# Attention and token mixer on one core: the two o visits of a straddling stretch, and the bank that the second one opens

## The chip, the core and the metric

The kernel runs on one core of a Trainium2 chip. The core has five engines with a queue each: TensorE (PE, matmuls; its weight loads are shown apart as PEld), VectorE (DVE), ScalarE (ACT), GpSimd (POOL) and SyncE (SP, which issues the DMAs). Matmuls write PSUM, which has eight banks of 128 x 512 fp32 values; only DVE and ACT read it here. The metric is the device time of one execution in microseconds, the median of three runs.

## The reference

Two branches over the same x (2048 x 640), mixed by a gate for each row. Cut to what matters:

```python
# A: 32 heads of 20, one shared k and v
q = (x @ wq).reshape(B, S, H, Dh).transpose(0, 2, 1, 3); k = x @ wk; v = x @ wv
p = softmax(einsum("bhqd,bkd->bhqk", q, k) * Dh ** -0.5)
a = einsum("bhqk,bkd->bhqd", p, v).transpose(0, 2, 1, 3).reshape(B, S, H * Dh) @ wo
# B: token mixer
u = gelu(einsum("bsd,sf->bdf", layernorm(x), w1) + b1)
b = (einsum("bdf,fs->bds", u, w2) + b2).transpose(0, 2, 1)
g = sigmoid((x * gate_w).sum(-1, keepdims=True))
out = g * a + (1 - g) * b          # S = 2048, D = 640, F = 1728
```

## The kernel before

After a prologue (layer norm, projections, the first B columns) one long loop does the rest. Attention is cut into 32 **query groups** n (four heads by 512 queries) and 16 key blocks kb of 128 keys; a **unit** in the code's list `units` is one pair (n, kb), 512 in all. For each unit there are four score matmuls (`qk`, line 668), each of which fills one PSUM bank; ACT reads the bank and writes the exponentials into an SBUF tile `p` (line 674). A **visit** (`pv_mm`, line 701) then multiplies the four p tiles of a unit by v and adds the products into the four 32-partition quarters of one bank, the o bank. The profile counts eight matmul records for a visit. Visits of kb 0 to 15 add into the same bank; the visit with kb = 0 starts it afresh, and after kb = 15 ACT copies it to SBUF (line 714, `on<-o`). The rest of that evacuation (transposes, division, a split in two, DMAs) is put off in the list `later` and handed out by `settle`, a piece at a time. When the text below says that a visit "opens the next group", it means a visit with kb = 0; the change's title calls the group of sixteen visits a unit.

The row maxima of a later group are computed ahead with the same kind of matmul (`ms_next`, line 479), each into one bank that DVE reduces (line 482).

**Banks.** Score and row maximum matmuls take banks in turn from `next_bank`: three of the pool `ps_m` (name `ms`) and three of `ps_s` (name `s`), alternately, so each bank comes round after six matmuls. `ring[0]` is the bit that alternates. A call makes a new tile in a pool's oldest slot, and its first writer waits until the old tile's reader is done. The seventh bank is `ps_g` for the matmuls of branch B and of the output projection (`g`), the eighth is `ps_o` for o.

**Order.** The program order is written out by hand. The loop runs over 326 **stretches** (`ph`, function `main`). Even and odd stretches use opposite halves of the PE rows: scores and maxima of half b are interleaved with some 15 to 17 `g` matmuls of the other half, so that two row halves work at once. A visit uses all 128 rows and four groups of 32 columns instead. An even stretch ends with one visit, an odd one with two back to back: three visits in two stretches (below: a **pair** of stretches). So `vs` holds one or two units, and `wide` says that it holds two. Since 16 is no multiple of 3, the two visits of an odd stretch are kb = 15 of one group and kb = 0 of the next every 48 units: units 15 and 16, 63 and 64, and so on to 447 and 448, ten times. There `parted` is true, and the first visit is moved to the middle of the stretch (line 1066), so that ACT can copy the o bank while the second half of the stretch runs and the second visit can open the same bank at its end.

The last 24 visits come after the loop in blocks of two, with four banks for scores (`s_banks`) and three for the projection's last jobs (`a_free`).

Of the kernel before, what the change touches and what calls it, by code (L numbers as in the profile page):

```python
# [9 lines left out]
F32 = mybir.dt.float32  # L10
# [7 lines left out]
P = 128  # L18
S, D, H, DH, F = 2048, 640, 32, 20, 1728
NS = S // P  # L20
# [4 lines left out]
NB = 512  # L25
# [14 lines left out]
def mix_kernel(ctx: ExitStack, tc: tile.TileContext, A_x, A_wq, A_wk, A_wv, A_wo,  # L40
# [5 lines left out]
    def f32(ap):  # L46
        return ap.bitcast(F32)
# [402 lines left out]
    ps_m = ctx.enter_context(tc.tile_pool(name="ps_m", bufs=3, space=PSUM))  # L450
# [6 lines left out]
    ring = []  # L457

    def next_bank():
        if not ring:  # L460
            return ps_m.tile([P, NB], F32, name="ms")
        ring[0] ^= 1
        return ps_m.tile([P, NB], F32, name="ms") if ring[0] else ps_s.tile([P, NB], F32, name="s")
    given = [0, 0]
    issued = [0, 0]

    def ms_next(b):
        k = given[b]
        if k >= 32 * NU:
            return None  # L470
        given[b] += 1
        n, r = divmod(k, 32)
        (kq, pr), qt = divmod(r // 4, 2), r % 4

        def step():
            if n not in mtiles:
                mtiles[n] = mpool.tile([P, 16, 4], F32, name="mp")
            ms = next_bank()
            nc.tensor.matmul(ms, qmax[n][64 * b:64 * b + 60, pr, qt * P:(qt + 1) * P],  # L479
                             kst[64 * b:64 * b + 60, kq * NB:(kq + 1) * NB], start=True, stop=True)  # L480
            c = (2 * b + pr) * 4 + qt
            nc.vector.tensor_reduce(mtiles[n][:, c, kq:kq + 1], ms, axis=AX.X, op=ALU.max)  # L482
            issued[b] += 1
            if min(issued) == 32 * n + 1:
                new_qmax(n + 1)

        return step
# [18 lines left out]
    def fetch_max(n):  # L506
        src = m_scr[n].rearrange("(i j b r) e -> j b r i e", j=2, b=2, r=8)
        for b in range(2):
            for j in range(2):
                rows = f32(qtiles[n][64 * b + 60 + j:64 * b + 61 + j])  # L510
                nc.sync.dma_start(out=rows.rearrange("o p (t i e) -> o (p t) i e", i=4, e=32), in_=src[j, b][None])
# [48 lines left out]
    def pop_chain():  # L560
        f = chain.pop(0) if chain else None
        if f:
            f()
# [39 lines left out]
    ps_s = ctx.enter_context(tc.tile_pool(name="ps_s", bufs=3, space=PSUM))  # L603
    ps_o = ctx.enter_context(tc.tile_pool(name="ps_o", bufs=1, space=PSUM))
# [24 lines left out]
    units = [(n, kb) for n in range(NU) for kb in range(NS)]  # L629
# [8 lines left out]
    s_banks, s_turn, a_free = [], [0], []  # L638
# [6 lines left out]
    def s_next(b):  # L645
        j = sc[b]
        if j >= 2 * len(units):
            return None
        sc[b] += 1

        def step():
            qk(j // 2, j % 2, b)

        step.score = True
        return step
# [36 lines left out]
    otile = {}  # L692
    later = []

    def pv_mm(u):
        n, kb = units[u]
        if kb == 0:
            otile[0] = ps_o.tile([P, NB], F32, name="o")
        o = otile[0]
        for hh in range(4):  # L700
            nc.tensor.matmul(o[32 * hh:32 * hh + 32, :], v_sb[:, kb, :], ptiles.pop((u, hh)),  # L701
                             start=(kb == 0), stop=(kb == NS - 1), skip_group_check=True)
        if kb == NS - 1 and n < NU - 1:
            qb, g = divmod(n, NQ)
            ot = ev.tile([P, NB // 32, 32], F32, name="ot")
            rl = ev.tile([P, NB // 32], F32, name="rl")
            on = ev.tile([P, NB], F32, name="on")
            oh = ev.tile([P, NB], F32R, name="oh")
            ol = ev.tile([P, NB], F32R, name="ol")
            direct = spare[0]  # L710
            src = o
            if not direct:
                src = on
                nc.scalar.activation(src, o, AF.Copy)

            def turn():
                nc.vector.transpose(ot.rearrange("p c e -> p (c e)"), src)

            def scale():
                if not direct:  # L720
                    turn()
                nc.vector.reciprocal(rl, ot[:, :, DH])  # L722
                (nc.vector if spare[0] else nc.gpsimd).tensor_mul(ot, ot, rl[:, :, None].to_broadcast([P, NB // 32, 32]))  # L723

            if direct:
                turn()

            def back():
                nc.vector.transpose(on, ot.rearrange("p c e -> p (c e)"))

            def high():
                nc.gpsimd.tensor_copy(oh, on)

            def low():
                nc.gpsimd.tensor_sub(ol, on, f32(oh))
                for j, t in enumerate((oh, ol)):
                    for hh in range(4):
                        r = (4 * g + hh) * DH
                        nc.sync.dma_start(out=o_scr[j, r:r + DH, qb * NB:(qb + 1) * NB],
                                          in_=f32(t[32 * hh:32 * hh + DH, :]))  # L740

            if direct:
                later.append((False, None))
            later.extend(((True, scale), (True, back), (False, high), (False, low)))
# [268 lines left out]
    def merged(lx, lf):  # L1013
        lanes, at, out = (list(lx), list(lf)), [0.0, 0.0], []
        while lanes[0] or lanes[1]:
            k = 0 if lanes[0] and (not lanes[1] or at[0] <= at[1]) else 1
            us, f = lanes[k].pop(0)
            if f:
                out.append(f)
            at[k] += us  # L1020
        return out
# [5 lines left out]
    def settle(wide=False):  # L1027
        for _ in range(2 if spare[0] else 1):
            if later and (wide or spare[0] or not later[0][0]):
                f = later.pop(0)[1]  # L1030
                if f:
                    f()
        pop_chain()
# [6 lines left out]
    def main(k, vs):  # L1040
        b = k % 2
        fs, rest, done = ph[k]
        fill = [(F_US, f) for f in fs] + [(0.0, f) for f in [signal] + done]
        if not vs:
            lx = [(3 * X_US, ms_next(b)), (3 * X_US, ms_next(b)), (X_US, s_next(b)), (X_US, ms_next(b))]
            lx += [(X_US, s_next(b)) for _ in range(3)]
            lf = fill + [(X_US, s_next(1 - b))]
        else:
            sx, sf = (MANY if len(fs) > 15 else FEW)[len(vs) == 1]
            lx = [(X_US, (s_next if c == "s" else ms_next)(b)) for c in sx]  # L1050
            lf = []
            for c in sf:
                lf += fill if c == "F" else [(X_US, (s_next if c == "s" else ms_next)(1 - b))]
        order = merged(lx, lf)
        scores = [f for f in order if getattr(f, "score", False)]
        known, kept = set(row_max), set(sent)
        wide = len(vs) == 2
        parted = wide and units[vs[0]][1] == NS - 1
        hold = None
        if done and vs and not k + 1 >= len(ph) and k % 2 == 0 and len(fs) > 15:  # L1060
            hold = [i for i, f in enumerate(order[:order.index(done[0])]) if f in scores][-1]
        for i, f in enumerate(order):
            if wide and i == (len(order) + 1) // 2:
                settle()
                if parted:
                    pv_mm(vs[0])
            if i == hold:
                delayed.append(None)
            f()
            if hold is not None and f is done[0]:  # L1070
                delayed.pop(1)()
                delayed.clear()
        ms_done()
        spare[0] = len(row_max) == NU
        settle(wide and not parted)
        if vs:
            n, kb = units[vs[0]][0] + 1, units[vs[0]][1]
            if n in kept and n not in back_in:
                fetch_max(n)
                back_in.add(n)  # L1080
        for f in rest:
            f()
        if vs and kb > 4 and n in known and n not in sent and n < NU:
            store_max(n)
            sent.add(n)
        for v in vs[parted:]:
            pv_mm(v)

    ring.append(0)
    v = 0  # L1090
    for k in range(len(ph)):
        n = 0 if k == 0 else 1 + k % 2
# [8 lines left out]
    if NU - 1 not in sent:  # L1101
        store_max(NU - 1)

    s_banks.extend(ps_s.tile([P, NB], F32, name="s") for _ in range(3))
    s_banks.append(ps_m.tile([P, NB], F32, name="ms"))
    a_free.append(ps_g.tile([P, NB], F32, name="g"))
    a_free.extend(ps_m.tile([P, NB], F32, name="ms") for _ in range(2))
    assert not later
    for i in range(4):
        tail_load(NS - 4 - NA + i, late=True)  # L1110
# [1 line left out]
    for n in BLOCKS:  # L1112
# [3 lines left out]
        i = 0  # L1116
# [31 lines left out]
    o = otile[0]  # L1148
# [78 lines left out]
```

## Time and profile before

| | |
|---|---|
| median of three runs | 1662.53 us (1661.41 to 1663.34) |
| profiled execution | 1662.79 us, of which 1661.0 us are the span from the first to the last instruction |
| DVE busy | 1431.1 us, 86% of the span |
| ACT busy | 1188.1 us, 72% |
| POOL busy | 608.1 us, 37% |

The profile is that of one execution. An engine's busy time is the union of its instructions; a chain of waits follows the last instruction back through whatever released it. A timeline row gives the start, the length, the engine, the line, the tiles (written<-read), the shapes, the count, and in brackets the idle time of that engine ahead of it with what ended it. A row of a window table gives the bounds, the length, the busy time (and number of records) of the engines, the granted clock, the DMA share and GB/s.

### The profile page before, as it was taken

The numbers are of one execution on the slowest core, as the hardware profiler recorded it, in microseconds if no ns is written. First come the engines' busy times: TensorE is split into PE (matmuls) and PEld (weight loads), VectorE is DVE, ScalarE is ACT, GpSimd is POOL, SyncE is SP. The second block draws the span as 40 slices with busy tenths as digits, with TensorE's granted clock in tenths as the row PEclk, the third lists the DMA queues.
The fourth block names the chain that finished last, engine by engine and source line by source line (L and its number), as shares of the span: only waits on it lengthen the run. The fifth ranks groups of instructions, "written<-read, shape, count | busy, mean of one in ns | idle before, by whom it ended". The sixth has DMA issues, their size and how long they took to land.

```text
span 1661.0 us, 38834 instructions
## 1 busy us (share of the span) xinstructions
PE 1651.6 (99%) x14877; PEld 1104.0 (66%) x14877; DVE 1431.1 (86%) x2725; ACT 1188.1 (72%) x2349; POOL 608.1 (37%) x765
## 2 busy tenths in 40 slices
PE   9999999999999999999999999999999999999998
PEld 7889666666666666666666666666666666666655
DVE  6689889989989999998999899899899989988943
ACT  4444777777777777777777777777777777777775
POOL 6568545544464554522232322122222221111220
PEclk9999999999999999999999999999999999999999
DMA  7655222222233222222222222122221222333521
GB/s 210 206 168 144 75 70 68 78 64 78 60 78 78 71 74 68 58 72 67 67 75 61 58 65 67 56 66 67 67 61 55 67 66 64 99 107 97 165 82 38
DMA packets 178527, 138.60 MB, mean 83 GB/s; under 512 B 33369, under 2 KB 144118, under 8 KB 178342
## 3 DMA queue, kind: packets, MB, share of 16 engines
q1 hardware_dynamic: 178054, 135.80, 29.3%
q8 instruction: 117, 1.92, 0.5%
q14 instruction: 68, 0.56, 0.1%
q10 hardware_dynamic: 288, 0.33, 0.1%
HBM read 102.36 MB, written 31.65 MB: 81 GB/s over the span
## 4 chain that ended last, share of the span: by engine, by line
PE 97%; DVE 2%; ACT 1%; issue 0%; DVEq 0%; ACTq 0%
PE o L701 29%; PE ms L479 19%; PE s L668 14%; PE g L763 10%; PE g L952 7%; PE ms L668 4%; PE pp L298 4%; PE g L898 3%; PE pu L586 2%; PE s L479 2%; DVE mp L482 1%; ACT p L674 1%; PE pp L362 0%; PE pt L290 0%; PE ms L853 0%; DVE yo L529 0%
## 5 line engine op out<-in xcount | busy, mean ns | idle before, releaser
L482 DVE TENSOR_REDUCE mp<-ms 128x1 f32<-128x512 f32 x1576 | 1003.2, 685 | 129.9 <-PE ms L479 105.0
L674 ACT ACTIVATE p<-s 128x512 f32<-128x512 f32 x1551 | 845.6, 606 | 307.2 <-PE s L668 292.4
L479 PE MATMUL ms<-kst,qmx 60*128 60x512 f32 x1576 | 673.7, 433 | 2.6 <-DVE mp L482 2.6
L668 PE MATMUL s<-qst,kst 62*128 62x512 f32 x1551 | 612.3, 400 | 0.0
L701 PE MATMUL o<-p,v_sb 128*32 128x512 f32 x4096 | 511.4, 601 | 0.0
L479 PEld LDWEIGHTS ms<-kst,qmx 60*128 60x128 f32 x1576 | 290.6, 185 | 264.1 <-ACT p L674 109.4
L482 DVE TENSOR_REDUCE mp<-s 128x1 f32<-128x512 f32 x472 | 315.9, 684 | 8.5 <-PE s L479 8.3
L668 PEld LDWEIGHTS s<-qst,kst 62*128 62x128 f32 x1551 | 286.2, 186 | 43.7 <-DVE flag L688 23.5
L674 ACT ACTIVATE p<-ms 128x512 f32<-128x512 f32 x497 | 286.4, 600 | 39.2 <-PE ms L668 36.7
L952 PE MATMUL g<-slot,wh 64*128 64x320 f32 x1280 | 297.6, 312 | 0.0
L129 POOL TENSOR_TENSOR wl<-wr,wh 128x512 fp32r<-128x512 f32 x176 | 228.0, 1297 | 47.8 <-PE g L763 21.1
L701 PEld LDWEIGHTS o<-p,v_sb 128*32 128x32 f32 x4096 | 97.6, 108 | 184.6 <-issue 176.7
L952 PEld LDWEIGHTS g<-slot,wh 64*128 64x128 f32 x1280 | 211.6, 184 | 2.0 <-issue 1.7
L479 PE MATMUL s<-kst,qmx 60*128 60x512 f32 x472 | 208.2, 448 | 0.4 <-DVE yo L525 0.4
L763 PE MATMUL g<-slot,wh 64*128 64x320 f32 x864 | 201.5, 313 | 0.0
L763 PE MATMUL g<-u,wh 64*128 64x320 f32 x864 | 201.0, 313 | 0.0
L668 PE MATMUL ms<-qst,kst 62*128 62x512 f32 x497 | 199.9, 402 | 0.0
L952 PE MATMUL g<-slot,wl 64*128 64x320 f32 x640 | 199.6, 312 | 0.0
L128 POOL CAST wh<-wr 128x512 fp32r<-128x512 f32 x144 | 88.0, 611 | 222.5 <-PE g L763 114.5
L763 PEld LDWEIGHTS g<-slot,wh 64*128 64x128 f32 x864 | 143.3, 184 | 1.7 <-issue 1.7
L723 POOL TENSOR_TENSOR ot<-ot,rl 128x512 f32<-128x512 f32 x30 | 31.5, 1050 | 307.3 <-DVE rl L722 307.3
L763 PEld LDWEIGHTS g<-u,wh 64*128 64x128 f32 x864 | 143.1, 184 | 1.1 <-issue 1.1
(221 smaller groups left out, 2086.2 us busy)
## 6 DMA issues: line engine op xcount, KB each, us to landing
wr<-in_B_w_dram SPq DMA_DIRECT2D x152, 256.0 KB
qmx<-q_scr SPq DMA_DIRECT2D x192, 80.0 KB
qst<-q_scr SPq DMA_DIRECT2D x192, 80.0 KB
slot<-o_scr SPq DMA_DIRECT2D x22, 320.0 KB
y_scr<-yo SPq DMA_DIRECT2D x16, 320.0 KB
o_scr<-oh SPq DMA_DIRECT2D x124, 40.0 KB
o_scr<-ol SPq DMA_DIRECT2D x124, 40.0 KB
q_scr<-qh SPq DMA_DIRECT2D x19, 256.0 KB
```

Source lines behind the costliest of these rows:

```text
L128: nc.gpsimd.tensor_copy(wh, wr)
L129: nc.gpsimd.tensor_sub(wl, wr, f32(wh))
L298: nc.tensor.matmul(pp, w, t, start=first and n == 0, stop=not more and n == len(steps) - 1)
L479: nc.tensor.matmul(ms, qmax[n][64 * b:64 * b + 60, pr, qt * P:(qt + 1) * P], kst[64 * b:64 * b + 60, kq * NB:(kq + 1) * NB], start=True, s ...
L482: nc.vector.tensor_reduce(mtiles[n][:, c, kq:kq + 1], ms, axis=AX.X, op=ALU.max)
L586: nc.tensor.matmul(pu[r][:, :HD2], w[rows, c, :], h[rows, st, :], start=(st == 0 and k == 0), stop=(st == NS - 1 and k == 2))
L668: nc.tensor.matmul(s, kst[64 * b:64 * b + 62, kb * P:(kb + 1) * P], q[64 * b:64 * b + 62, pr, :], start=True, stop=True)
L674: nc.scalar.activation(p, s, AF.Exp, scale=SCALE)
L701: nc.tensor.matmul(o[32 * hh:32 * hh + 32, :], v_sb[:, kb, :], ptiles.pop((u, hh)), start=(kb == 0), stop=(kb == NS - 1), skip_group_check ...
L763: other_tile(half, nc.tensor.matmul(hold["p"][:, :HD2], w[r, fc % HS, :], u[d][r, fc, :], start=(hold["n"] == 1), stop=(hold["n"] == 6 * F ...
L898: other_tile(half, nc.tensor.matmul(hold["p"][:, :HD2], o[r, c, :], w[r, c, d * HD2:(d + 1) * HD2], start=(hold["n"] == 1), stop=(hold["n" ...
L952: other_tile(half, nc.tensor.matmul(hold["p"][:, :HD2], w[r, st % HS, :], h[d][r, st, :], start=(hold["n"] == 1), stop=(hold["n"] == 6 * NS)))
```

## The change

The ring becomes a list of six lasting tiles that are rotated, in place of new tiles from two pools. `otile[0]` is one tile as well, allocated once. In a wide stretch whose second visit has kb = 0, that visit calls `pv_mm` with `swap`: the present o bank goes to the young end of the ring, the oldest bank of the ring becomes the o bank. The parted form, with its visit in the middle of a stretch, is gone, and both visits stand at the end as in every other wide stretch. After the loop the six banks of the ring are handed to `s_banks` and `a_free` in the order of their age.

```diff
     def next_bank():
         if not ring:
             return ps_m.tile([P, NB], F32, name="ms")
-        ring[0] ^= 1
-        return ps_m.tile([P, NB], F32, name="ms") if ring[0] else ps_s.tile([P, NB], F32, name="s")
+        ring.append(ring.pop(0))
+        return ring[-1]
...
-    def pv_mm(u):
+    def pv_mm(u, swap=False):
         n, kb = units[u]
-        if kb == 0:
-            otile[0] = ps_o.tile([P, NB], F32, name="o")
+        if swap:
+            ring.append(otile[0])
+            otile[0] = ring.pop(0)
         o = otile[0]
...
         wide = len(vs) == 2
-        parted = wide and units[vs[0]][1] == NS - 1
...
             if wide and i == (len(order) + 1) // 2:
                 settle()
-                if parted:
-                    pv_mm(vs[0])
...
-        settle(wide and not parted)
+        settle(wide)
...
-        for v in vs[parted:]:
-            pv_mm(v)
-
-    ring.append(0)
+        for v in vs:
+            pv_mm(v, wide and v == vs[1] and units[v][1] == 0)
+
+    ring.extend((ps_s if i % 2 else ps_m).tile([P, NB], F32, name="s" if i % 2 else "ms") for i in range(6))
+    otile[0] = ps_o.tile([P, NB], F32, name="o")
...
-    s_banks.extend(ps_s.tile([P, NB], F32, name="s") for _ in range(3))
-    s_banks.append(ps_m.tile([P, NB], F32, name="ms"))
+    s_banks.extend(ring[:4])
     a_free.append(ps_g.tile([P, NB], F32, name="g"))
-    a_free.extend(ps_m.tile([P, NB], F32, name="ms") for _ in range(2))
+    a_free.extend(ring[4:])
```

## The prediction

> **What bounds the kernel now.** I read the engines' busy times first, then the chain of waits, then the timeline around single visits, and windows cut at visits.
>
> ```profile
> PE 1651.6 (99%) x14877; PEld 1104.0 (66%) x14877; DVE 1431.1 (86%) x2725; ACT 1188.1 (72%) x2349; POOL 608.1 (37%) x765
> ...
> PE 97%; DVE 2%; ACT 1%; issue 0%; DVEq 0%; ACTq 0%
> ```
>
> PE is busy for 99% of the span and carries 97% of the chain that ended last. A busy PE need not be a well used one: one row half can stand still while the other works, and the record shows no idle time. So PE's time has to be read as a pace, from one visit to the next. The timeline of PE shows a normal wide stretch (16 records of o in a row) and one of the ten straddling ones:
>
> ```profile
> 211.07 1.92 PE L701 MATMUL o<-p,v_sb 128*32 128x512 f32 x16
> ...
> 218.41 1.07 PE L701 MATMUL o<-p,v_sb 128*32 128x512 f32 x8
> ...
> 220.85 1.07 PE L701 MATMUL o<-p,v_sb 128*32 128x512 f32 x8
> ```
>
> Two visits back to back take 1.92 us, two apart 2 x 1.07 = 2.14. To see the whole price I cut windows from the start of an even stretch's visit to the start of the next even stretch's: a pair of stretches with three visits (24 records). The view is that of windows for line 701 alone; the length of a window is the pace. The ten straddling pairs:
>
> ```profile
> 215.82:224.89 9.07, 3.20 (x24) 0.47 (x24) 1.00 0.23 65
> 354.84:363.78 8.94, 3.20 (x24) 0.47 (x24) 1.00 0.16 47
> 493.73:502.67 8.94, 3.20 (x24) 0.47 (x24) 1.00 0.11 29
> 632.60:641.66 9.07, 3.20 (x24) 0.47 (x24) 1.00 0.25 56
> 772.21:781.41 9.21, 3.20 (x24) 0.47 (x24) 1.00 0.22 66
> 912.27:921.35 9.08, 3.19 (x24) 0.47 (x24) 1.00 0.46 133
> 1052.14:1061.08 8.94, 3.20 (x24) 0.47 (x24) 1.00 0.30 84
> 1191.92:1200.99 9.08, 3.20 (x24) 0.47 (x24) 1.00 0.24 56
> 1331.88:1340.81 8.94, 3.20 (x24) 0.47 (x24) 1.00 0.01 2
> 1470.05:1479.30 9.24, 3.20 (x24) 0.47 (x24) 1.00 0.34 97
> ```
>
> And pairs that do not straddle: first 15 of them in one window (360 records), then five single ones, then two of the last stage (the output projection):
>
> ```profile
> 224.89:354.84 129.95, 44.84 (x360) 8.63 (x360) 1.00 0.28 73
> 816.39:825.05 8.66, 2.99 (x24) 0.57 (x24) 1.00 0.29 85
> 868.65:877.46 8.81, 2.99 (x24) 0.57 (x24) 1.00 0.26 72
> 1096.06:1104.72 8.65, 2.99 (x24) 0.57 (x24) 1.00 0.31 84
> 1148.32:1157.13 8.81, 2.99 (x24) 0.58 (x24) 1.00 0.24 70
> 1288.27:1296.93 8.66, 2.99 (x24) 0.57 (x24) 1.00 0.29 68
> 1505.18:1513.77 8.59, 2.99 (x24) 0.57 (x24) 1.00 0.39 116
> 1513.77:1522.46 8.69, 2.99 (x24) 0.58 (x24) 1.00 0.20 56
> ```
>
> The granted clock is 1.00 in all of them, so the difference is not the clock. The kernel keeps a beat that the straddling pairs break. The five single windows lie at the same place of their five-pair job in the second B stage as the straddling pairs at 772, 912, 1052, 1192 and 1332, in this order; the place decides whether the beat there is 8.66 or 8.81. All five hold one of the other two kinds of group end (kb = 15 as the single visit, or as the second of a wide stretch), so an o copy as such does not break the beat in that stage.
>
> **The change, part by part.** *The visit in the middle goes.* A straddling pair should take the length of a pair without it. The first four go against 129.95 / 15 = 8.663: 9.07 + 8.94 + 8.94 + 9.07 - 4 x 8.663 = 1.37. The next five, each against its own place: 0.55, 0.27, 0.29, 0.27 and 0.28, together 1.66. The last against 8.59: 0.65, or 0.55 if a group's end costs its 0.10 there as in the window at 1513.77. Sum 1.37 + 1.66 + 0.65 = **3.68 us**, at least 3.58.
>
> The plain price is some 0.28 us: 0.22 for the parted visits, and the rest, as I take it, because one row half runs out before the other at one more place. The Trainium skill, TensorEngine Tiling (Array Packing), Key Properties, says that a change of tiling mode drains TensorE; its TensorE: Matmul & The Clock Gate, Single matmul latency, puts a drain at about 175 ns. My estimate from that page is 2 x 0.175 = 0.35 us for each additional excursion and 3.5 us for ten; the rows have 0.28 at the plain sites, below it, and more at others, and the measurement decides.
>
> At four sites more is lost. At the first, the timeline of ACT and the rows of line 952 around it say why:
>
> ```profile
> 219.57 0.60 ACT L714 ACTIVATE on<-o 128x512 f32<-128x512 f32 x1 [0.40 <-PE o L701]
> ...
> 221.49 0.55 ACT L519 ACTIVATE yo<-g,bias 128x320 f32<-128x320 f32 x1
> ```
>
> ```profile
> L952 PEldq EVENT_SEMAPHORE  x1: 321/321/321, 221.8 to 221.8; - x1
> ```
>
> The o copy in the middle of the stretch pushes ACT back by 0.6 us and its wait; then ACT empties the g bank only until 222.04, and the next job's first g matmul holds PE's queue for 0.32 us. With the copy behind the visits, the g bank is emptied ahead of it, so this goes too; it is already in the sum.
>
> *The o copy moves* behind the first visit. Above, ACT starts it 219.57 - 218.41 = 1.16 us after the visit's start. It would run from 1.16 to 1.76 us after the start of two joined visits. That time has to be free on ACT; where the last stage is busiest, ACT, DVE and PE show:
>
> ```profile
> 1386.96 1.10 ACT L674 ACTIVATE p<-ms 128x512 f32<-128x512 f32 x2
> 1387.91 0.63 ACT L674 ACTIVATE p<-s 128x512 f32<-128x512 f32 x1
> 1390.43 2.09 ACT L674 ACTIVATE p<-ms 128x512 f32<-128x512 f32 x4 [1.89 <-PE ms L668]
> ```
>
> ```profile
> 1389.42 0.68 DVE L482 TENSOR_REDUCE mp<-s 128x1 f32<-128x512 f32 x1
> ```
>
> ```profile
> 1388.04 1.92 PE L701 MATMUL o<-p,v_sb 128*32 128x512 f32 x16
> ...
> 1390.95 0.40 PE L668 MATMUL ms<-qst,kst 62*128 62x512 f32 x1
> ```
>
> ACT idles 1.89 us, from 0.50 to 2.39 after the visits' start at 1388.04. The copy fits there with 0.63 to spare, so I cost it at nothing; without the cover it would hold the next exponentials back by up to 0.60. Nothing of `later` moves: in a stretch that straddles the list is empty, and its first piece is taken at the end of the next wide stretch in both forms. No DMA is added or moved.
>
> *The second visit takes a ring bank.* The oldest of six is read by ACT in this stretch; its read ends at 1388.06 (1386.96 + 1.10), 0.02 after the visits' start, while the second visit starts some 1.92 - 1.07 = 0.85 after it. No wait. The next matmuls find banks one turn younger. The fifth is the tight one: it takes the bank that DVE reads last, until 1389.42 + 0.68 = 1390.10, and starts at 1390.95, a margin of 0.85 us. The sixth takes the old o bank, emptied at 1.76. No wait, again at nothing; behind such a wait stand all of PE's matmuls, so each 0.1 us of it would cost 0.1.
>
> *Costs that no row shows.* First, whether two visits into two banks join as well as two into one: from 0 to what parting them costs, 0.22 x 10 = 2.1 us. I take 0, since all that the second needs is there by then. Second, waits that the six lasting tiles add or save, for some 3,900 matmuls. The nearest rows:
>
> ```profile
> L668 PEldq EVENT_SEMAPHORE  x130: 51/51/163, 170.8 to 1605.5; - x130
> ```
>
> ```profile
> L479 PEldq EVENT_SEMAPHORE  x54: 51/51/51, 97.8 to 1496.7; - x54
> ```
>
> ```profile
> L701 PEldq EVENT_SEMAPHORE  x1: 51/51/51, 176.0 to 176.0; - x1
> ```
>
> A wait of its own in PE's queue takes 51 ns. There are 184 on the ring's matmuls: if all go, and none was hidden, 184 x 0.051 = 9.4 us are gained; if each of 3,900 gets one, 199 us are lost. Between ends so far apart I go by the third row: the o tile is written 16 visits long as one lasting tile, and all 512 visits together have a single such wait. I take 0. Third, other bank orders at the start of the tail: between 0 and one read, 0.68; 0, as all banks are read during the visits before.
>
> **Sum:** 3.6 us, between the two forms of the last site. From the execution profiled, 1662.79 - 3.6 = 1659.2; the median of the runs is 0.26 lower, so **1658.9 us**.
>
> **The rivals.** *A: the visits do not join.* A wait or a pause ahead of the new bank parts them, though they stand together: 2.1 of 3.6 us are lost, 1662.5 - 1.5 = 1661.0. For it: no row shows o going into two banks back to back. Against: matmuls of lines 479 and 668 change banks each time at full pace. Chance 0.10.
>
> *B: the time is taken by another engine*, and nothing is gained: 1662.5. The Trainium skill, TensorEngine Tiling (Array Packing), PSUM Bottleneck, warns that emptying PSUM may become the limit once tiles speed up TensorE; here that would be DVE. Against it: DVE is busy for 86% of the span, and the 15 pairs above keep 8.66 with no more DVE time to spare than a mended pair would have. Chance 0.06.
>
> *C: slower, by waits on the lasting tiles.* If a tile that is written again makes PE wait in its queue where a new tile did not, on all ring matmuls, and one in 20 of these 51 ns is not covered by the other row half, 199 / 20 = 10 us are lost and 3.6 gained: 1669. It turns slower from 3.6 / 0.051 = 71 open waits on. For it: 184 such rows exist today. Against: the o tile's single one. Chance 0.06.
>
> **How the numbers follow.** The forecast has 0.78. A measurement of this kernel can tell 0.2%, 3.3 us, from no change; the three runs lie within 1 us of their median, so a median moves by about half of that. 3.6 lies only 0.3 above the bound: of 0.78 I put 0.57 beyond it and 0.21 inside. A falls inside but for 0.01, B inside, C slower. Faster 0.58, same 0.36, slower 0.06. The range runs from 1657.7 (the whole 3.68, a low median, some waits saved) to 1661.2, which takes in A; B and C are left out with the rest of the tails, 0.2 in all.
>
> **What would show it.** Right: 16 records of o in a row in all wide stretches, where ten now have two times 8; ten straddling pairs of 8.66 or 8.81, the last of 8.59 to 8.69; the o copy within 1.2 us of the first visit's start, in ACT's idle time; no idle on PE ahead of the second visit; the g wait of 0.32 us gone at the first site. Wrong: a pair above 8.75 in the first B stage, a joined visit longer than 1.92, more event rows on the score lines (C), or a pace above 8.66 in pairs that do not straddle.

## The result, and the profile after

The changed kernel takes 1657.85 us (median of 14 runs, 1656.71 to 1660.62) against 1661.95 for the one before, timed beside it (14 runs, 1660.80 to 1664.11): 4.1 us less, a ratio of 0.9978 with a 95% interval of 0.9970 to 0.9985. The forecast was 1658.9, a gain of 3.6, in a range of 1657.7 to 1661.2.

The head of the page of the changed kernel:

```profile
span 1658.8 us, 38824 instructions
...
PE 1647.2 (99%) x14877; PEld 1103.4 (67%) x14877; DVE 1432.4 (86%) x2725; ACT 1188.1 (72%) x2349; POOL 608.9 (37%) x765
```

PE still bounds it, and is busy 4.4 us less; DVE, ACT and POOL do the same work as before. The span fell by only 2.2 us, and the reason lies ahead of the visits. The view of the visits' line (701 before, 702 now) gives when visits started first and last; here are the row of the kernel before and that of the changed kernel, for the bank that takes the first visit:

```profile
L701 PE MATMUL o<-p,v_sb x4096: 592/592/618, 176.4 to 1648.9; 128*32 128x512 f32 x196
```

```profile
L702 PE MATMUL o<-p,v_sb x512: 592/592/617, 178.3 to 1195.7; 128*32 128x512 f32 x171
```

The first visit starts at 176.4 in the profile before and at 178.3 in this one. The profiled execution is the slowest of its 14 (1660.62), and it lost 1.9 us in the prologue, which the change does not touch; in profiles of the experiments below the first visit starts between 174.5 and 177.7. From the first visit to the end, 1661.0 - 176.4 = 1484.6 us became 1658.8 - 178.3 = 1480.5: 4.1 us less, as the medians have it.

The ten straddling pairs of stretches, in the same windows as before (from one even stretch's visit to the next, line 702 alone):

```profile
217.66:226.31 8.65, 2.99 (x24) 0.57 (x24) 1.00 0.29 79
356.23:364.88 8.66, 2.99 (x24) 0.57 (x24) 1.00 0.21 53
494.84:503.50 8.66, 2.99 (x24) 0.58 (x24) 1.00 0.11 30
633.42:642.07 8.65, 2.99 (x24) 0.58 (x24) 1.00 0.31 73
772.57:781.23 8.66, 2.99 (x24) 0.57 (x24) 1.00 0.27 82
912.23:921.02 8.80, 2.99 (x24) 0.57 (x24) 1.00 0.49 141
1051.83:1060.48 8.66, 2.99 (x24) 0.57 (x24) 1.00 0.31 87
1191.29:1200.10 8.81, 2.99 (x24) 0.57 (x24) 1.00 0.25 58
1330.93:1339.59 8.66, 2.99 (x24) 0.57 (x24) 1.00 0.01 2
1468.49:1477.07 8.58, 2.99 (x24) 0.57 (x24) 1.00 0.34 105
sum 86.79, PE 29.89 PEld 5.75; mean PE 2.99 PEld 0.57
```

Every pair has the beat of its neighbours, and PE's time for the visits fell from 3.20 to 2.99 us in each. PE's timeline shows the two joined visits of the first pair, into two banks:

```profile
221.56 1.07 PE L702 MATMUL o<-p,v_sb 128*32 128x512 f32 x8
222.44 1.04 PE L702 MATMUL ms<-p,v_sb 128*32 128x512 f32 x8
```

The second starts 0.88 us after the first, and both are done 1.92 us after the first's start, as two visits into one bank are. The ten pairs took 90.50 us before and 86.79 now: 3.7 of the 4.1 us. Of the other pairs only two changed by more than 0.05 us: the one at 790 (8.66 before, 8.87 after) and the one at 1341 (8.61 before, 8.34 after), which is spoken of below.

### The profile page after: what moved, and what is told of

Read it like the earlier page. It is cut to its first block, busy times and chain, and to the rows that moved or that the text cites. A ratio compares the mean times of both kernels' runs of the same rounds, so it can differ in the third digit from the quotient of the medians.

```text
span 1658.8 us, 38824 instructions
## 1 busy us (share of the span) xinstructions
PE 1647.2 (99%) x14877; PEld 1103.4 (67%) x14877; DVE 1432.4 (86%) x2725; ACT 1188.1 (72%) x2349; POOL 608.9 (37%) x765
## 3 DMA queue, kind: packets, MB, share of 16 engines
q8 instruction: 117, 1.92, 0.5%
## 4 chain that ended last, share of the span: by engine, by line
PE 95%; DVE 3%; DMA 1%; SPq 1%; ACT 1%; issue 0%; POOL 0%; DVEq 0%; ACTq 0%
PE ms L702 15%; PE s L702 11%; PE s L479 10%; PE g L764 10%; PE ms L479 9%; PE s L668 8%; PE ms L668 8%; PE g L953 7%; PE o L702 4%; PE pp L298 3%; PE o L479 3%; PE g L899 3%; PE o L668 2%; PE pu L586 2%; DVE mp L482 1%; ACT p L674 0%
## 5 line engine op out<-in xcount | busy, mean ns | idle before, releaser
L482 DVE TENSOR_REDUCE mp<-s 128x1 f32<-128x512 f32 x892 | 583.9, 685 | 62.2 <-PE s L479 51.8
L482 DVE TENSOR_REDUCE mp<-ms 128x1 f32<-128x512 f32 x878 | 574.7, 684 | 59.3 <-PE ms L479 48.7
L674 ACT ACTIVATE p<-ms 128x512 f32<-128x512 f32 x887 | 497.7, 603 | 161.3 <-PE ms L668 152.1
L674 ACT ACTIVATE p<-s 128x512 f32<-128x512 f32 x875 | 489.3, 605 | 148.4 <-PE s L668 134.9
L479 PE MATMUL s<-kst,qmx 60*128 60x512 f32 x892 | 390.5, 438 | 0.4 <-DVE yo L525 0.4
L479 PE MATMUL ms<-kst,qmx 60*128 60x512 f32 x878 | 375.0, 436 | 3.6 <-DVE mp L482 3.6
L668 PE MATMUL s<-qst,kst 62*128 62x512 f32 x875 | 334.5, 402 | 0.0
L702 PE MATMUL ms<-p,v_sb 128*32 128x512 f32 x2048 | 255.0, 600 | 0.0
L482 DVE TENSOR_REDUCE mp<-o 128x1 f32<-128x512 f32 x278 | 190.3, 685 | 13.1 <-PE o L479 9.1
L702 PE MATMUL s<-p,v_sb 128*32 128x512 f32 x1536 | 192.0, 600 | 0.0
```

The costliest lines, as they stand in the source:

```text
L668: nc.tensor.matmul(s, kst[64 * b:64 * b + 62, kb * P:(kb + 1) * P], q[64 * b:64 * b + 62, pr, :], start=True, stop=True)
L674: nc.scalar.activation(p, s, AF.Exp, scale=SCALE)
```

## The experiments

All are timed against the kernel before; intervals are 95%. Edits are shown against the changed kernel. The straddling sites are named by the unit of their first visit: 15, 63, 111, 159, 207, 255, 303, 351, 399, 447.

### The lasting tiles alone

The parted stretch comes back, nothing is swapped; the ring of six tiles stays.

```diff
+        parted = wide and units[vs[0]][1] == NS - 1
...
+                if parted:
+                    pv_mm(vs[0])
...
-        settle(wide)
+        settle(wide and not parted)
...
-        for v in vs:
-            pv_mm(v, wide and v == vs[1] and units[v][1] == 0)
+        for v in vs[parted:]:
+            pv_mm(v)
```

> The ring of six lasting tiles and the one o tile alone; the first visit of a straddling stretch stays in the middle and nothing is swapped. Theory (joining the visits makes the whole gain): as before, 1662 +- 0.6 us, the straddling pairs 8.94 and 9.07 as before. Rival (the lasting tiles save waits in PE's queue): 1658, with the straddling pairs still at 8.94.

Measured: 1661.0 us against 1661.25, ratio 0.9998 (0.9989 to 1.0007). No pair at a straddling site differs from the one before by as much as 0.03 us. The event rows of the score lines, in PE's queue:

```profile
L668 PEldq EVENT_SEMAPHORE  x130: 51/51/51, 169.0 to 1603.5; - x130
```

Still 130, as in the kernel before (and in the changed kernel). Lasting tiles neither add nor save waits here; rival C of the prediction falls, and with it any gain from the tiles.

### The swap with parted visits

As above, but the second visit takes the oldest bank (`pv_mm(v, parted)`).

> The swap is kept, but the first visit is back in the middle of the stretch. Theory (the gain is from visits that stand together): as before, 1662 +- 0.6 us; straddling pairs 8.94 plain and 9.07 at the first and fourth. Rival (before, the second visit or what follows it waited for the o bank, and the new bank alone is the gain): 1658, pairs of 8.66.

Measured: 1661.69 us, ratio 0.9999 (0.9990 to 1.0008). The windows of sites 15 and 63:

```profile
215.81:224.89 9.07, 3.19 (x24) 0.47 (x24) 1.00 0.24 62
354.87:363.80 8.93, 3.20 (x24) 0.47 (x24) 1.00 0.16 45
```

They, and the other eight, are those of the kernel before. A free bank for o is worth nothing by itself; before the change, the middle of the stretch had already hidden the o copy.

### Joined visits without the swap

```diff
-            pv_mm(v, wide and v == vs[1] and units[v][1] == 0)
+            pv_mm(v)
```

> Both visits at the end of the stretch, but into one o bank: the second has to wait for ACT's copy. The copy ends 1.76 us after the first visit's start, so the second starts at about 1.82 in place of 0.86. Theory: 0.97 us more for each of the ten pairs than in the changed kernel, a plain pair 9.63, in all 1657.9 + 9.7 = 1667.6 us, slower than before by 5.6. Rival (the wait is hidden, the new bank is not needed): 1658.

Measured: 1668.89 us, ratio 1.0041 (1.0028 to 1.0053). The timelines of PE and of ACT at site 63:

```profile
359.33 1.07 PE L702 MATMUL o<-p,v_sb 128*32 128x512 f32 x8
361.13 1.06 PE L702 MATMUL o<-p,v_sb 128*32 128x512 f32 x8 [0.74 <-ACT on L715]
```

```profile
360.46 0.62 ACT L715 ACTIVATE on<-o 128x512 f32<-128x512 f32 x1
```

The copy starts 1.13 us after the first visit, and the second visit stands behind it until 1.80 after that start, where 1.82 was expected; the window of this pair is the second of these, 9.62 against 9.63 expected:

```profile
215.30:225.49 10.19, 3.20 (x24) 0.47 (x24) 1.00 0.35 90
355.42:365.04 9.62, 3.20 (x24) 0.47 (x24) 1.00 0.25 72
```

The first is site 15, where a job of B ends, 0.57 dearer. ACT's timeline of the changed kernel at that place shows what stands ahead of the copy: the emptying of the g bank (line 519), and behind it the next step of the gelu (line 522, 222.94 to 223.41).

```profile
222.36 0.55 ACT L519 ACTIVATE yo<-g,bias 128x320 f32<-128x320 f32 x1
...
223.32 0.58 ACT L715 ACTIVATE on<-o 128x512 f32<-128x512 f32 x1
```

The copy starts 1.76 us after the visits (at 221.56) in place of 1.13, and whoever waits for it waits that much longer. Site 159 has the same job end and costs the same; the two make up most of what the run took beyond the 1667.6 us expected. So joining the visits is possible only with the second bank. The two halves of the change are worth nothing or less each, and 4 us together.

### The late copy

The swap with parted visits, and the o copy no longer in the middle of the stretch but at its end (`parted` and the end of `settle` as in the two runs before).

```diff
-    def pv_mm(u, swap=False):
+    put_off = []
+
+    def pv_mm(u, swap=False, late=False):
...
-                nc.scalar.activation(src, o, AF.Copy)
+                copy = lambda: nc.scalar.activation(src, o, AF.Copy)
+                put_off.append(copy) if late else copy()
...
+                    pv_mm(vs[0], late=True)
...
+        while put_off:
+            put_off.pop(0)()
+        for v in vs[parted:]:
+            pv_mm(v, parted)
```

> As the run with the swap and the parted visits, but the o copy is issued at the end of the stretch, ahead of the second visit, and no longer in its middle. Theory (the four dear sites pay for ACT's copy that delays the emptying of the g bank, the rest pays for parting): the excess of the sites at 15, 159, 207 and 447 falls to the plain 0.28, the other six stay; 0.14 + 0.14 + 0.27 + 0.37 = 0.9 us less than before, 1661.1, pairs of 8.94 at the first four sites. Rival (parting itself is dearer at those four places): 1662, the first and fourth pair stay at 9.07.

Measured: 1661.62 us, ratio 0.9999 (0.9990 to 1.0008). That interval alone could not tell a gain of 0.9 us from none; the windows can. The ten pairs take 90.30 us, only 0.2 less than before. Sites 15, 207 and 447:

```profile
214.67:223.71 9.04, 3.20 (x24) 0.47 (x24) 1.00 0.23 61
771.32:780.36 9.04, 3.20 (x24) 0.47 (x24) 1.00 0.22 66
1469.04:1478.29 9.25, 3.20 (x24) 0.47 (x24) 1.00 0.31 97
```

Sites 15 and 159 fell by 0.03, 207 by 0.17, 447 not at all. Much of the extra stays when the copy leaves the middle, and the rows around site 15 begin to say why. The wait ahead of the first g matmul behind the second visit, ACT, and PE:

```profile
L956 PEldq EVENT_SEMAPHORE  x1: 207/207/207, 220.6 to 220.6; - x1
```

```profile
220.24 0.54 ACT L519 ACTIVATE yo<-g,bias 128x320 f32<-128x320 f32 x1
...
221.19 0.58 ACT L717 ACTIVATE on<-o 128x512 f32<-128x512 f32 x1
...
222.62 0.61 ACT L674 ACTIVATE p<-o 128x512 f32<-128x512 f32 x1
```

```profile
219.71 1.06 PE L704 MATMUL ms<-p,v_sb 128*32 128x512 f32 x8
220.70 0.50 PE L479 MATMUL s<-kst,qmx 60*128 60x512 f32 x1
220.88 0.38 PE L956 MATMUL g<-slot,wh 64*128 64x320 f32 x1
```

With the copy out of the way ACT has emptied the g bank at 220.78, 0.11 us sooner behind the visit than in the kernel before. Behind a lone visit the next matmuls start after 1.0 us, at 220.70, so g comes 0.18 late still, where it was 0.29 late before. In the changed kernel the same wait is longer, not shorter:

```profile
L953 PEldq EVENT_SEMAPHORE  x1: 527/527/527, 222.4 to 222.4; - x1
```

It runs from 222.4 to 222.9, below the joined visits that keep PE busy from 221.56 to 223.48, and costs nothing. What two joined visits give at the end of a job is **cover**: some 1.85 us of PE work whose inputs ACT and DVE have already delivered, where a lone visit gives 1.0.

The late copy has a price of its own at sites 15 and 159, so this run does not cleanly remove the copy there. It now runs behind the gelu, and the exponentials behind it come 0.2 us later than in a stretch without a copy: ACT reads the score bank `o` until 223.23, and only then do the weights for the last row maximum, which takes that bank, load (223.28).

At site 447 another engine is late. DVE of the kernel before sets the flag that the next g matmul of the other row half waits for; it stands behind the row maxima. DVE, and PE's next matmuls:

```profile
1476.47 0.69 DVE L482 TENSOR_REDUCE mp<-s 128x1 f32<-128x512 f32 x1
1476.49 0.06 DVE L688 MEMSET flag<- 1x1 f32 x1
```

```profile
1475.11 1.06 PE L701 MATMUL o<-p,v_sb 128*32 128x512 f32 x8
1476.10 0.50 PE L668 MATMUL ms<-qst,kst 62*128 62x512 f32 x1
1476.72 0.38 PE L898 MATMUL g<-slot 64*128 64x320 f32 x1
```

The flag comes 1.4 us after the lone visit's start: too late for the 1.0 that it covers, in time for 1.85. In the changed kernel it comes as late behind the visits (1474.05 against 1472.60), and g starts with the other matmuls at 1474.46. The next run puts lone visits where there is no copy.

### Parting all the other wide stretches

```diff
+        joined = wide and units[vs[0]][1] == NS - 1
+        parted = wide and not joined
...
+                if parted:
+                    pv_mm(vs[0])
...
-        for v in vs:
-            pv_mm(v, wide and v == vs[1] and units[v][1] == 0)
+        for v in vs[parted:]:
+            pv_mm(v, joined and v == vs[1])
```

> The changed kernel, but in the 153 wide stretches that do not straddle the first visit goes to the middle of the stretch; no o copy and no swap is added there. Theory now (parting costs 0.28 us for a second excursion wherever it is; besides, two joined visits cover 1.85 us in which ACT empties the g bank and DVE sets the flag, one visit only 1.0): plain pairs 8.94, pairs with the end of a B job some 9.04, each of the 26 parted pairs of the last stage 8.59 + 0.65 = 9.24; in all 153 x 0.28 + 35 x 0.10 + 26 x 0.37 = 56 us more than 1657.9, 1714. Rival 1 (the dear sites pay for the o copy): no extra without a copy, 153 x 0.28 = 43, 1701, last stage 8.87. Rival 2 (parting costs only where a group ends): 1658.

Measured: 1740.1 us, ratio 1.0467 (1.0452 to 1.0481): 82 us more than the changed kernel, where 56 were expected. Windows of seven parted pairs, none with an o copy in the middle: two of the first B stage with an extra DVE step, the first with the end of a B job and the second without; one with the end of a B job and no such step; the first and second pair after a group end; one of the second B stage with the end of a job; and one of the last stage:

```profile
190.93:199.96 9.03, 3.20 (x24) 0.47 (x24) 1.00 0.01 2
337.13:346.16 9.03, 3.19 (x24) 0.47 (x24) 1.00 0.39 110
355.09:364.03 8.94, 3.20 (x24) 0.47 (x24) 1.00 0.24 68
226.53:236.15 9.62, 3.20 (x24) 0.47 (x24) 1.00 0.16 38
236.15:245.53 9.37, 3.19 (x24) 0.47 (x24) 1.00 0.11 28
940.99:950.03 9.05, 3.20 (x24) 0.47 (x24) 1.00 0.25 75
1511.64:1520.84 9.21, 3.19 (x24) 0.47 (x24) 1.00 0.30 86
```

Plain pairs came out as expected, 8.94 (8.66 + 0.28), and so did the last stage, 9.21, without a copy: there the lone visit is the cause. The ends of B jobs came out in two ways. In the second stage g starts 1.27 us behind the lone visit and the pair takes 9.05, 0.11 beyond the plain price. In the first stage g starts after 1.18 us, as late as in the run with the late copy:

```profile
L953 PEldq EVENT_SEMAPHORE  x1: 207/207/207, 361.0 to 361.0; - x1
```

Yet this pair, the third of the windows, takes 8.94, and the eight pairs of the first stage that have a job's end but neither a group end nor the extra DVE step at that place take 8.94 to 8.96: that much lateness costs nothing. The 9.03 of the first window is not the job's end, since the second has none and costs the same; in both DVE combines a group's maxima (line 493, 0.22 us) 1.5 us behind the visit, and the row maxima behind it come 0.1 us late. The one pair of the first stage that has a job's end and a copy behind the gelu, that of units 78 and 79, takes 9.04, as sites 15 and 159 did with the late copy.

So at 15 and 159 a job's end alone costs nothing (8.94 to 8.96 here), a copy alone costs nothing (8.94 at 63 and 111), and the two together cost 0.13: there the copy is needed for the extra. At 207 the copy makes 0.17 of the 0.27 and the lone visit the rest; at 447 the lone visit makes all of 0.37.

The 26 us too many come from the pairs behind a group end, which the expectation had left out: 9.62 and 9.37 in place of 8.94, 1.1 us more for each of 30 ends, 33 us in all. Job ends and the last stage brought some 7 us beside it, where 13 were expected. The timeline of DVE and of PE in the first of these pairs:

```profile
232.94 0.70 DVE L718 STREAM_TRANSPOSE ot<-on 128x512 f32<-128x512 f32 x1
...
233.85 3.10 DVE L482 TENSOR_REDUCE mp<-s 128x1 f32<-128x512 f32 x5
```

```profile
231.58 1.06 PE L702 MATMUL ms<-p,v_sb 128*32 128x512 f32 x8
...
234.53 0.49 PE L668 MATMUL s<-qst,kst 62*128 62x512 f32 x1 [0.22 <-DVE mp L482]
```

There `settle` hands DVE the transpose of o and the reciprocal at the end of the wide stretch, 0.95 us, and in the second pair the transpose back, 0.70; under two joined visits they cost PE nothing (8.66 for this pair in the changed kernel), behind a lone one the row maxima come late and PE waits for their banks. It is the same cover once more.

### How much room the ring has

Two runs (the first diff the one, the second the other) turn the ring of the changed kernel after each of the 153 other wide stretches (the expectations say 152): by one bank, so that the next matmuls find it as young as after a swap, and by five, so that the next matmul takes the bank used last.

```diff
             pv_mm(v, wide and v == vs[1] and units[v][1] == 0)
+        if wide and units[vs[1]][1]:
+            ring.append(ring.pop(0))
```

```diff
             pv_mm(v, wide and v == vs[1] and units[v][1] == 0)
+        if wide and units[vs[1]][1]:
+            ring.insert(0, ring.pop())
```

> The changed kernel, but after the visits of each of the 152 other wide stretches the ring is turned by one bank without a use, so that the next five matmuls find banks one turn younger, as after a swap. Theory (the banks are read during the visits; margin 0.76 us by the timeline of the changed kernel): 1657.9 +- 0.6, no pair longer. Rival (a bank out of the ring is paid for later): 0.1 us or more for each, 1673 or more.

> The changed kernel, but after the visits of the 152 other wide stretches the next matmul takes the bank that was used last. Theory (PE waits as soon as that bank's read ends later than the first matmul after the visits, 1.85 us from their start): no cost before the last stage, where the read ends at up to 1.2 to 1.5; in the last stage, where DVE ends it at 2.06, 0.27 us in each of 26 pairs, 7 us, 1665. Rival (such waits are hidden by the other row half): 1658.

Measured: by one bank 1659.2 us, ratio 0.9982 (0.9973 to 0.9991), against the changed kernel's 0.9978 (0.9970 to 0.9985), which it can't be told from; the kernel before, timed beside it, took 1662.48. By five it was 1666.39, ratio 1.0025 (1.0015 to 1.0035). Windows of the run by five, 15 pairs of the first B stage and four of the last stage:

```profile
224.37:354.27 129.90, 44.83 (x360) 8.62 (x360) 1.00 0.28 72
1435.55:1471.11 35.56, 11.96 (x96) 2.30 (x96) 1.00 0.43 113
```

The first stage keeps its 8.66 even so. In the last, 35.56 / 4 = 8.89 against 8.59: 0.30 us for each of these pairs, and 0.27 in the mean of the 27 pairs of that stage, as expected. PE's timeline in one of them shows the wait:

```profile
1439.66 1.92 PE L702 MATMUL s<-p,v_sb 128*32 128x512 f32 x16
1441.77 0.50 PE L668 MATMUL ms<-qst,kst 62*128 62x512 f32 x1 [0.18 <-DVE mp L482]
```

The first matmul behind the visits starts 2.11 us after them, where the changed kernel has 1.85. The wait for a bank is real and fully paid where a read ends too late, and the margin behind the visits is as wide as the timeline said: one bank out of the ring costs nothing that can be measured.

### The copy behind both visits

`late` and `put_off` are as in the late copy.

```diff
         for v in vs:
-            pv_mm(v, wide and v == vs[1] and units[v][1] == 0)
+            joined = wide and units[vs[1]][1] == 0
+            pv_mm(v, joined and v == vs[1], joined and v == vs[0])
+        while put_off:
+            put_off.pop(0)()
```

> The changed kernel with the o copy behind both visits in place of between them, at the ten straddling sites. Theory (behind the first visit it fits in ACT's idle time; behind the second it runs from 2.0 to 2.6 us and delays the next exponentials, as at the other group ends): pairs before the last stage stay at 8.66 and 8.81, the one at 447 goes from 8.58 to 8.69; in all 0.1 us. Rival (ACT is late there anyhow, or the copy's place does not matter): 447 stays at 8.58.

Measured: 1656.97 us in a single run, and the pair at 447 has 8.62. But the experiment did not do what it was meant to: the copies start as long after the visits (1.13 to 1.76 us) as in the changed kernel. The order in the program moved the copy behind matmuls of another engine only; on ACT's own queue nothing changed places, and the copy waits for the first visit alone. What a later copy would cost was not tried.

## Why the prediction was right

**The frame held.** PE's pace sets the time, the straddling pairs break it, and mended pairs take the beat of the place they are at: 3.68 us forecast for the ten, 3.71 measured. The last site came out at 8.58, the better of its two values. The whole time came out 1.05 us below the forecast, near the low end of its range; 0.58 of that is the kernel before, whose median is 1661.95 in 14 runs where three had given 1662.53 (they lay within 1.12 us of it, not within 1), and the rest is a gain of 4.1 in place of 3.6. The order of the banks in the tail and the lasting tiles were costed at nothing, and the run with the tiles alone and the tail's unchanged pace (68.7 us from the first visit behind the loop to the end before, 68.6 after) bear it out.

**The plain price** of 0.28 us for an excursion of its own is confirmed at scale by the run that parts the other 153 stretches: 8.94 in the pairs of the first B stage that have nothing else in them. My estimate from the Trainium skill, TensorE: Matmul & The Clock Gate, Single matmul latency, 0.35, was too high.

**The joining** was right: two visits into two banks take the 1.92 us of two into one, and 2.99 us a pair, so rival A falls. Rival B falls as well, since DVE does the same work, 1432 us for 1431, in 4.1 us less.

**The ring's margin** was right, and the two turned rings put numbers on it.

**One step holds for half of its price: the cause of the extra at the four dear sites.** The prediction had it that "the o copy in the middle of the stretch pushes ACT back", and it let this stand for all four sites. The extra was in the sum with its right size, since that came from the windows and not from the cause; that the sum came out is no support for the cause. At 15 and 159 the mechanism stands: the copy puts the emptying of the g bank back by 0.11 us, so that g starts 0.29 late in place of 0.18, and only the former costs time (0.13 each). At 207 it makes 0.17 of 0.27. At 447 it makes nothing: there DVE's flag is late. In all the copy is behind some 0.4 of the 0.9 us; the other 0.5 is the cover that a lone visit lacks, at 207 and 447.

The prediction also had the g bank emptied ahead of the next g matmul once the copy moved. The g wait is there still and longer, 0.53 for 0.32 us, but under the visits. The o copy's place is off too: it starts 1.13 to 1.30 us after the first visit at eight sites, but 1.76 at 15 and 159, behind the gelu; the cover bears that as well.

**What stays open:** 0.4 us between the ten pairs and the whole. Of it, 0.27 is the pair at 1341, just behind the site at 399, and the pair at 790 takes 0.21 back; the rest is spread over many pairs, less than 0.05 us in each. At 1341, in the kernel before, the last row maximum ahead of the visits starts only at 1344.52, when ACT has read its bank (until 1344.47), 0.23 us after the one of the other row half; in the changed kernel the two start together. The pair is shorter by some 0.25 in the changed kernel, in the run that only joins the visits and in the two that only swap the bank, and not with the lasting tiles alone, so either half of the change is enough for it; why was not followed up. Slips of 0.2 us turn up in single pairs of most runs.

## What to carry to other kernels

Read a busy engine's pace from one recurring instruction to the next: a share of 99% hid ten places, 3.7 us in all, where its beat was slower. A block of work whose inputs are all there is also cover for whatever the other engines finish late, so splitting it can cost more than its own overhead: here nothing to 0.1 us where a bank is emptied late, and up to 0.7 where postponed work is handed out. An experiment that moves a suspect instead of removing it may only move its price, as the late copy did; look for a place that has the rest without the suspect. And when two edits are each needed for the other (joined visits and a second bank), try each alone before you say which one pays.

## What was not expected of the hardware

A wait in PE's queue is not yet a loss: the queue stood for 0.53 us ahead of a g matmul while the visits issued before it kept the array busy, and nothing was lost. Behind a lone visit, a g matmul that started 0.18 us late cost nothing, one 0.27 late cost 0.11 and one 0.43 late 0.27. And the time of the prologue, which is the same in all these kernels, varied by 3.8 us between profiles (first visit at 174.5 to 178.3), about as much as the change gains, so that a single execution's span would have told little.
